# Three edits to a fused attention, soft-MoE and cosine-gated MLP kernel: the order of work where each of its stages opens or closes

## The chip, the cores and the metric

The kernel runs on one core of a Trainium2 chip. The metric is device time in microseconds (us) of one execution. A core has five engines that run their own instruction queues and wait for each other through semaphores: TensorE (PE; its weight loads are listed apart as PEld), VectorE (DVE), ScalarE (ACT), GpSimd (POOL) and SyncE (SP), which here only issues DMAs.

## The reference

```python
# q, k, v: (4, 12, 448, 64)
scores = np.where(causal_mask, -1e9, (q @ k.T) / 8)
attn = softmax(scores)                       # rows
x = (attn @ v)  -> (1792, 768)               # tokens x model
logits = x @ phi                             # 32 slots
slot_input = softmax(logits, axis=0).T @ x
for e in range(8):                           # 4 slots each
    slot_out[e] = relu(slot_input[e] @ w1[e]) @ w2[e]
x = softmax(logits, axis=1) @ slot_out
h = x @ w_in                                 # w_in, w_out: float64 on the host
out = (h * cos(h)) @ w_out                   # 768 -> 2048 -> 768
```

## The kernel before

**Three stages.** Attention works on 24 pairs of heads (`pair_step(t)`, L472, called for t = 0 to 26 in the loop at L595). The piece stage (L745 to L780) streams the expert weights w1 and w2 as 48 pieces of 1 MB. The last stage (L782 to L1004) computes h, h*cos(h) and the product with w_out. The instructions of one engine run in the order in which the code issues them (`tc.manual_schedule()`).

**Attention.** For a pair t the step issues the score products `qk_mm(t, c)` (L287), c = 0 to 2, two heads each, into banks 0 to 3 of PSUM. A fourth, small block of scores, c = 3, of both heads together, lies in the last 64 columns of bank 0 and is issued one step ahead, `qk_mm(t + 1, 3)` at L527. Dependencies are kept per bank, so the score products of a pair wait until DVE has read the c = 3 block out of bank 0. `score` (L298) is a DVE instruction that adds the mask (`cs`, a tile of constants: identity in columns 0 to 127, masks in 192 to 703, `rep` in 704 to 831) and takes the row maximum; it returns a function that issues the exponential on ACT (L308). Then come `recip` (L312), `norm` (L319, on DVE or POOL), and a step later the transposes (L328), their copies (L179, L181) and the product with v (L360 to L369). Before the first pair, L583 to L594 issue the loads of pair 0, of `cs`, of v of pair 0, of pair 1 and of phi on SP, five memsets on DVE, and the c = 3 block of pair 0 with its exponential.

**keep_warm(n)** (L457) issues n products of the identity with itself into bank 3. Nothing reads them. In float32 each product is two matmul records with two weight loads; every float32 product of this kernel shows so.

**The piece stage.** `next_piece` (L726) issues loads as slots come free. After the pieces come the loads of the raw weights of the last stage, `ld(j)` (L674): an item j is one 768 KB block of w_in (even j) or w_out (odd j), 128 of the 2048 hidden columns, in float64. There are four raw buffers, so ld(j) waits until item j - 4 has been decoded. `decode` (L697) turns float64 into float32 with one ACT instruction (L684) and three DVE ones, l (L687), h (L691) and s (L695). Item 0 is decoded inside the piece loop (L739). After the last piece the loop copies its sums (ACT L773), issues keep_warm(2), transposes (L778) and copies the result to `soT` (DVE L779).

**The last stage.** For a group q of hidden columns: `w_mm` (L790, product of soT and w_in, PE), `w_4` (L800, ACT), `w_rep` (L804, PE), `w_s` (L807, ACT), `w_d` (L811, DVE). Then for each of 64 steps s, a step being 128 hidden columns for a block of 512 (or 256) tokens: H (L827, PE), Y (L831, ACT), R (L834, DVE), S (L837, ACT), G (L840, DVE), K (L843, ACT: the high part of g), L (L846, POOL: the low part), and `back(s, m)` (L848): for each of six output blocks m three matmuls, high weight by high g (L853), low by high (L854) and high by low (L855). The high and low parts of w_out are made from item 2c + 1 by u (`up_part`, ACT L706) and v (`lo_part`, POOL or DVE L719). F copies or adds finished sums (L861 to L865). `SEQ` (L30) gives the order of blocks and columns: step 0 needs column block 0, step 1 block 1, step 4 block 2, step 8 block 3.

**The planner.** The order in which the last stage is issued comes from a list scheduler in the kernel's own Python (L871 to L983). Each task has the engines it may run on with a cost, its predecessors, and a key (its due time in steps); `free` holds when each engine is free, all 0.0. At a moment each free engine takes the ready task with the lowest key, unless a more urgent one becomes ready soon. Loads are tasks of 1.87 us, `("so",)` stands for soT, ready at 3.0. The plan decides order only; on the chip each engine waits where an input is late. After it, `warm` (L991) adds 6, 5 and 12 identity products behind the first w_mm, w_rep and H.

## Time and profile before

| | us |
|---|---|
| median of three runs (558.65 to 562.61) | 560.85 |
| the profiled execution | 561.64 |
| its span, first to last instruction | 559.9 |
| busy in the span: PE | 516.5 |
| DVE | 369.7 |
| ACT | 318.6 |
| POOL | 159.2 |

All times in the rows are microseconds from the start of the span; mean durations are ns. The profiled execution's own time is 1.74 us above its span. A matmul record starts when its data enters the array and ends with a modelled end, so records of one engine overlap, and the distance from one start to the next is what an instruction costs in a stream.

### The profile page before, as it was taken

To read this page: it belongs to the slowest core of one execution; us is meant where nothing else is said; L and a number is where in the kernel's file an instruction comes from. 1 tells how busy PE (TensorE), PEld (TensorE's weight loads), DVE (VectorE), ACT (ScalarE), POOL (GpSimd) and SP (SyncE) were. 2 spreads that over 40 slices of the span, in tenths; PEclk is the share of its full clock that TensorE was granted. 3 is DMA by queue.
4 is the path that set the end of the run, shared out by engine and by line. 5 is a ranking of instruction groups with operands and counts; after the bars stand their busy time and mean duration, and the time that the engine had idled before them with its cause. 6 is when DMAs were issued, how large, how long until landed. Compare 5 with 4: busy or idle time off the path is not lost.

```text
span 559.9 us, 10301 instructions
## 1 busy us (share of the span) xinstructions
PE 516.5 (92%) x3794; PEld 387.3 (69%) x3794; DVE 369.7 (66%) x918; ACT 318.6 (57%) x737; POOL 159.2 (28%) x195
## 2 busy tenths in 40 slices
PE   4999999989999998887779989999989999999997
PEld 2777767767767763422457768777867878888997
DVE  3777777778777745001488888788888987635532
ACT  4888858857886712001375866565647646543452
POOL 1233333323323300000053624342423422232231
PEclk9999999999999999998789999999999999999999
DMA  5477547475645689999844141424226101303301
GB/s 180 167 258 258 184 155 252 172 248 179 235 166 219 248 325 414 420 418 420 332 156 176 50 170 60 167 76 151 101 72 221 57 10 48 112 1 113 114 1 57
DMA packets 23954, 100.28 MB, mean 179 GB/s; under 512 B 2656, under 2 KB 6624, under 8 KB 17760
## 3 DMA queue, kind: packets, MB, share of 16 engines
q1 hardware_dynamic: 23904, 99.63, 47.8%
q8 instruction: 30, 0.49, 0.3%
q14 instruction: 20, 0.16, 0.1%
HBM read 94.11 MB, written 5.51 MB: 178 GB/s over the span
## 4 chain that ended last, share of the span: by engine, by line
PE 51%; DMA 19%; DVE 13%; ACT 12%; issue 3%; SPq 0%; ACTq 0%; DVEq 0%
DMA w<-in_w_dram 10%; PE bank L853 8%; PE bank L854 8%; PE bank L855 8%; PE bank L295 7%; PE bank L328 5%; ACT p L308 5%; DMA zraw<-in_w_in_dram 5%; DMA zraw<-in_w_out_dram 4%; ACT pts L179 3%; DVE zscr L840 2%; PE bank L827 2%; PE bank L363 1%; DVE zfa L695 1%; PE bank L390 1%
## 5 line engine op out<-in xcount | busy, mean ns | idle before, releaser
L853 PE MATMUL bank<-zg,zhl 128*128 128x512 f32 (+1 forms) x384 | 142.4, 371 | 0.0
L855 PE MATMUL bank<-zg,zhl 128*128 128x512 f32 (+1 forms) x384 | 140.2, 365 | 0.4 <-POOL zg L846 0.4
L854 PE MATMUL bank<-zg,zhl 128*128 128x512 f32 (+1 forms) x384 | 140.3, 365 | 0.0
L846 POOL TENSOR_TENSOR zg<-zscr,zg 128x512 fp32r<-128x512 f32 (+1 forms) x64 | 81.6, 1278 | 155.4 <-ACT zg L843 124.3
L308 ACT ACTIVATE p<-p,pst 128x320 f32<-128x320 f32 (+3 forms) x168 | 87.6, 526 | 32.5 <-DVE pst L306 30.6
L325 POOL TENSOR_SCALAR p<-p,pst 128x320 f32<-128x320 f32 (+3 forms) x120 | 62.6, 539 | 131.2 <-ACT p L308 116.4
L853 PEld LDWEIGHTS bank<-zg,zhl 128*128 128x128 f32 x384 | 73.0, 190 | 12.7 <-issue 1.4
L855 PEld LDWEIGHTS bank<-zg,zhl 128*128 128x128 f32 x384 | 72.9, 190 | 12.7 <-POOL zg L846 0.9
L854 PEld LDWEIGHTS bank<-zg,zhl 128*128 128x128 f32 x384 | 73.0, 190 | 11.4
L306 DVE CUSTOM_DVE_ANT_0 p<-bank,cs 128x320 f32<-128x320 f32 (+3 forms) x168 | 66.9, 448 | 16.4 <-PE bank L295 12.6
L328 PE MATMUL bank<-cs,p 128*128 128x128 f32 (+1 forms) x456 | 59.8, 277 | 3.1 <-ACT pts L179 2.9
L834 DVE SCALAR_TENSOR_TENSOR zscr<-zscr,bank 128x512 f32<-128x512 int32 (+1 forms) x64 | 39.4, 618 | 34.1 <-ACT zscr L831 33.7
L837 ACT ACTIVATE zscr<-zscr,b_h 128x512 f32<-128x512 f32 (+1 forms) x64 | 42.6, 669 | 27.7 <-DVE zscr L834 27.5
L328 PEld LDWEIGHTS bank<-cs,p 128*128 128x128 f32 (+1 forms) x456 | 49.6, 134 | 11.3 <-issue 9.5
L840 DVE TENSOR_TENSOR zscr<-bank,zscr 128x512 f32<-128x512 f32 (+1 forms) x64 | 39.6, 621 | 22.0 <-ACT zscr L837 21.8
L295 PE MATMUL bank<-qk 64*128 64x192 f32 (+2 forms) x288 | 48.3, 471 | 5.4 <-DVE pst L306 5.4
L843 ACT ACTIVATE zg<-zscr 128x512 fp32r<-128x512 f32 (+1 forms) x64 | 36.8, 576 | 28.6 <-DVE zscr L840 28.3
L831 ACT ACTIVATE zscr<-bank,b_q 128x512 int32<-128x512 f32 (+1 forms) x64 | 40.2, 630 | 22.1 <-PE bank L827 21.9
L295 PEld LDWEIGHTS bank<-qk 64*128 64x128 f32 x288 | 27.2, 196 | 26.3 <-issue 10.3
L179 ACT ACTIVATE pts<-bank 128x512 f32<-128x512 f32 x71 | 40.5, 591 | 3.8 <-PE bank L328 2.3
L684 ACT ACTIVATE zraw<-zraw 128x768 f32<-128x768 f32 x32 | 28.9, 910 | 23.4 <-DMA zraw<-in_w_in_dram 15.6
L719 POOL TENSOR_TENSOR zhl<-uacc,zhl 128x768 fp32r<-128x768 f32 x4 | 8.8, 2204 | 98.6 <-ACT zhl L706 98.6
(147 smaller groups left out, 692.6 us busy)
## 6 DMA issues: line engine op xcount, KB each, us to landing
w<-in_w_dram SPq DMA_DIRECT2D x48, 1024.0 KB, 6.9
zraw<-in_w_in_dram SPq DMA_DIRECT2D x16, 768.0 KB, 5.0
zraw<-in_w_out_dram SPq DMA_DIRECT2D x16, 768.0 KB, 4.4
qk<-in_qk_dram SPq DMA_DIRECT2D x24, 480.0 KB, 4.2
xk<-in_v_dram SPq DMA_DIRECT2D x12, 256.0 KB, 2.6
out_dram<-zps SPq DMA_DIRECT2D x8, 256.0 KB, 2.0
xts<-in_v_dram SPq DMA_DIRECT2D x12, 128.0 KB, 2.1
lt<-in_v_dram SPq DMA_DIRECT2D x12, 128.0 KB, 2.2
```

The source lines that it names most:

```text
L179: ACT.activation(o, i, AF.Copy)
L295: PE.matmul(sreg(j, c), lhsT=Q(p)[h, q0:q0 + 128], rhs=K(p)[h, 0:ln], start=True, stop=True)
L306: DVE.tensor_tensor_reduce(out=dst, in0=sb, in1=m, scale=-0.125, scalar=3.0e38, op0=ALU.add, op1=ALU.min, accum_out=st_[:, col:col + 1])
L308: return pr(f"exp{j}{c}")(lambda: ACT.activation(dst, dst, AF.Exp, bias=st_[:, col:col + 1], scale=-1.0, accum_out=st_[:, 8 + col:9 + col]))
L325: ENG[CFG["norm"][3 * j + c if c < 3 else 6]].tensor_scalar(dst, dst, st_[:, 24 + col:25 + col], 0.0, op0=ALU.mult, op1=ALU.add)
L328: PE.transpose(out, src, by)
L837: ACT.activation(y_(s), y_(s), AF.Sin, bias=b_h, scale=1.0)
L840: DVE.tensor_tensor(y_(s), hb[:, 0:n_(s)], y_(s), ALU.mult)
L846: eng.tensor_tensor(g_(s)[1], y_(s), g_(s)[0].bitcast(F32), ALU.subtract)
L853: PE.matmul(o, lhsT=wh, rhs=gh, start=first, stop=False)
L854: PE.matmul(o, lhsT=wl, rhs=gh, start=False, stop=False)
L855: PE.matmul(o, lhsT=wh, rhs=gl, start=False, stop=last)
```

## The change

Three edits. (1) In attention, the c = 3 block of pair 0 no longer comes first: the three main score products of pair 0 do, after eight identity products on a zeroed part of `uacc` into bank 7. Inside step 0, the c = 3 blocks of pairs 0 and 1 and the load of pair 2 are issued at new places, with 6 and 4 such products behind them. The load of `cs` becomes three, masks first. (2) In the piece loop, three identity products follow each of the pieces that are counted 42 to 47, and `decode(1)` is issued after the last piece, ahead of the copy that leads to soT. (3) The planner of the last stage starts from times at which the engines, soT and the first raw items are ready; loads cost 2.4 instead of 1.87; keys of w_in items are 0.7 step later; the twelve tasks from the first w_mm to the first output product (`CHN`) are a chain, and PE, ACT and DVE refuse any other task that would run past the moment at which the chain next needs that engine; identity products fill PE's gaps in the chain; and step 0's output products run as three passes over the six blocks (high by high; low by high; high by low), each pass with its own inputs.

```diff
-    def keep_warm(n):
+    def keep_warm(n, t=cs):
         for _ in range(n):
-            PE.matmul(bank[3][:, 0:128], lhsT=ident, rhs=ident, start=True, stop=True)
+            PE.matmul(bank[3 if t is cs else 7][:, 0:128], lhsT=t[:, 0:128], rhs=t[:, 0:128], start=True, stop=True)
...
-        if t + 2 < NPAIR:
+        if 0 < t < NPAIR - 2:
             load_raw(t + 2)
         sc(0, 0)
+        if t == 0:
+            qk_mm(0, 3)
+            keep_warm(6, uacc)
+            load_raw(2)
...
+        if t == 0:
+            e3 = score(0, 0, 3)
         sc(0, 1)
         sc(1, 1)
         e(1, 0)
+        if t == 0:
+            e3()
...
         sc(1, 2)
+        if t == 0:
+            qk_mm(1, 3)
+            keep_warm(4, uacc)
+            f3 = score(1, 0, 3)
...
-        if nxt:
+        if nxt and t:
             qk_mm(t + 1, 3)
...
-            e3 = score(t + 1, 0, 3)
+            e3 = score(t + 1, 0, 3) if t else f3
...
-        SP.dma_start(cs, cst)
+        SP.dma_start(cs[:, 192:704], cst[:, 192:704])
+        SP.dma_start(cs[:, 0:192], cst[:, 0:192])
+        SP.dma_start(cs[:, 704:832], cst[:, 704:832])
...
-        qk_mm(0, 3)
-        score(0, 0, 3)()
+        DVE.memset(uacc[:, 0:128], 0.0)
+        keep_warm(8, uacc)
...
+                    if 42 <= npc[0] < 48:
+                        keep_warm(3)
+                if npc[0] == 48:
+                    decode(1)
                 ACT.activation(so, sb[:, 0:256], AF.Copy)
                 tb = bank[6]
                 if npc[0] == 48:
-                    keep_warm(2)
+                    keep_warm(1)
...
+    def back0(s, m):
+
+        k_ = (0, 1, None, None, None, 2)[m]
+        gh, gl = g_(0)
+        for m in range(6):
+            fc = seq[0][1]
+            PE.matmul(bank[m][:, 0:n_(0)], lhsT=w_blk(fc, int(k_ == 1), m), rhs=gl if k_ == 2 else gh, start=k_ == 0,
+                      stop=k_ == 2 and seq[0][3])
...
-        key = need[GRP[qof[c]][0]] - 2.2 if k_ == "i" else need[c] - 0
-        if j >= 1:
+        key = need[GRP[qof[c]][0]] - 1.5 if k_ == "i" else need[c] - 0
+        if j == 1:
+            task(("s", 1), dict(DMA=5.05), [], -2)
+        if j >= 2:
             if j >= NRAW:
-                task(("ld", j), dict(DMA=1.87), [("s", j - NRAW) if j > NRAW else None], j)
+                task(("ld", j), dict(DMA=2.4), [("s", j - NRAW) if j > NRAW else None], j)
...
-    task(("so",), dict(DMA=3.0), [], -1)
+    task(("so",), dict(DMA=5.199999999999999), [], -1)
...
+        if s == 0:
+            task(("B", 0, 0), dict(T=1.4), [("K", 0), ("u", 0)], .0)
+            task(("B", 0, 1), dict(T=1.4), [("B", 0, 0), ("v", 0)], .1)
+            task(("B", 0, 5), dict(T=1.4), [("B", 0, 1), ("L", 0)], .2)
...
-    free = dict.fromkeys("TADP", 0.0)
+    free = dict(T=6.0, A=5.6, D=5.95, P=3.0)
+    TIMED = {("so",): 0, ("s", 1): 0, ("raw", 2): 0, ("raw", 3): 0}
+    for t, x in ((("raw", 2), 4.9), (("raw", 3), 6.8)):
+        T[t] = (dict(DMA=x - .9),) + T[t][1:]
+    CHN = [("wm", 0), ("w4", 0), ("wr", 0), ("ws", 0), ("wd", 0), ("H", 0), ("Y", 0), ("R", 0), ("S", 0), ("G", 0), ("K", 0), ("B", 0, 0)]
+    isch = set(CHN)
+
+    def chain_next(e, now):
+        # returns when the first unplanned task of CHN that runs on e is expected to be ready
...
+                if e in "TAD" and t not in isch and chain_next(e, now) < now + eng[e] - 0.05:
+                    continue
...
+                if e == "T" and ("wm", 0) in done and ("B", 0, 0) not in done and chain_next("T", now) > now + .3 and \
+                        not any(w_ < now + .3 and "T" in T[x][0] for w_, x in soon):
+                    plan.append((now, len(plan), ("kw",), e))
+                    free["T"] = now + .23
...
-    warm = {("wm", 0): 6, ("wr", 0): 5, ("H", 0): 12}
...
+            if t[0] == "kw":
+                keep_warm(1)
+                continue
```

(The comment line in `chain_next` stands for its body, which walks the chain with the planner's own costs.)

## Rows read from the trace of the kernel before

**Rows 1.** The chain that ended last, share of the span by line.
```profile
DMA w<-in_w_dram 10%; PE bank L853 8%; PE bank L854 8%; PE bank L855 8%; PE bank L295 7%; PE bank L328 5%; ACT p L308 5%; DMA zraw<-in_w_in_dram 5%; DMA zraw<-in_w_out_dram 4%; ACT pts L179 3%; DVE zscr L840 2%; PE bank L827 2%; PE bank L363 1%; DVE zfa L695 1%; PE bank L390 1%
```
**Rows 2.** Windows: length, busy PE, PEld, DVE, ACT, POOL (instructions), PE clock, DMA share, GB/s.
```profile
27.50:34.65 7.15, 6.82 (x57) 5.17 (x57) 5.61 (x23) 5.80 (x19) 2.59 (x6) 1.00 0.74 253
...
288.40:336.40 48.00, 44.71 (x223) 35.01 (x224) 41.75 (x54) 33.81 (x54) 21.18 (x14) 0.96 0.37 132
...
368.80:460.00 91.20, 86.72 (x450) 68.66 (x449) 78.89 (x108) 52.69 (x81) 30.45 (x21) 1.00 0.28 98
```
**Rows 3.** Timeline of the opening: start, duration, engine, line, instruction, idle before.
```profile
1.55 0.06 DVE L592 MEMSET b_h<- 128x1 f32 x1
...
3.99 0.69 PE L290 MATMUL bank<-qk 128*128 128x64 f32 x2 [3.99 <-DMA qk<-in_qk_dram]
...
5.68 3.50 PE L295 MATMUL bank<-qk 64*128 64x448 f32 x12 [1.00 <-DVE pst L306]
...
12.08 3.31 PE L295 MATMUL bank<-qk 64*128 64x448 f32 x12 [2.54 <-DVE pst L306]
...
20.57 1.89 PE L295 MATMUL bank<-qk 64*128 64x448 f32 x12 [0.18 <-DVE pst L306]
```
**Rows 4.** Windows with the granted clock, columns as in rows 2.
```profile
12.50:13.00 0.50, 0.50 (x4) 0.28 (x2) 0.33 (x2) 0.00 (x0) 0.50 (x2) 0.50 0.53 180
...
16.00:16.50 0.50, 0.50 (x7) 0.50 (x5) 0.50 (x3) 0.28 (x1) 0.00 (x0) 1.00 0.25 54
...
288.00:292.00 4.00, 3.75 (x10) 2.98 (x11) 3.38 (x6) 3.82 (x7) 3.01 (x3) 0.61 0.51 197
```
**Rows 5.** DMA issues from 2.0 to 2.5: the load of pair 1, us to landing.
```profile
qk<-in_qk_dram SPq DMA_DIRECT2D x1, 480.0 KB, 6.2
```
**Rows 6.** DMA issues from 253 to 254 (at 253.77): item 1, us to landing.
```profile
zraw<-in_w_out_dram SPq DMA_DIRECT2D x1, 768.0 KB, 19.2
```
**Rows 7.** Timeline from the last piece to the first output product.
```profile
271.26 1.89 PE L771 MATMUL bank<-w,dk 128*4 128x256 f32 x16 [0.71 <-DMA w<-in_w_dram]
...
273.08 0.93 PEld L459 LDWEIGHTS bank<-cs 128*128 128x128 f32 x4 [0.86 <-issue]
...
273.27 0.38 ACT L773 ACTIVATE cs<-bank 128x256 f32<-128x256 f32 x1 [9.19 <-PE bank L771]
273.56 0.89 ACT L684 ACTIVATE zraw<-zraw 128x768 f32<-128x768 f32 x1
...
274.76 0.19 DVE L779 COPY dT<-bank 128x32 f32<-128x32 f32 x1 [7.85 <-PE bank L778]
...
275.01 0.71 PE L794 MATMUL bank<-zfa,dT 128*32 128x128 f32 x12 [0.28 <-DVE dT L779]
275.53 0.96 DVE L691 SCALAR_TENSOR_TENSOR uacc<-zraw,uacc 128x768 int32<-128x768 int32 x1
...
275.77 0.28 ACT L802 ACTIVATE cs<-bank 128x128 f32<-128x128 f32 x1
...
278.78 2.60 POOL L719 TENSOR_TENSOR zhl<-uacc,zhl 128x768 fp32r<-128x768 f32 x1 [84.51 <-ACT zhl L706]
...
280.04 1.76 DVE L687 TENSOR_SCALAR lt<-zraw 128x768 int32<-128x768 int32 x1
...
284.04 0.29 DVE L813 TENSOR_TENSOR zWS<-bank,zWS 32x128 fp32r<-32x128 f32 x1 [1.52 <-ACT zWS L809]
...
284.38 0.49 PE L827 MATMUL bank<-CT,zWS 96*128 96x512 f32 x1 [0.69 <-DVE zWS L813]
...
285.29 0.68 ACT L831 ACTIVATE zscr<-bank,b_q 128x512 int32<-128x512 f32 x1
...
288.23 0.63 ACT L843 ACTIVATE zg<-zscr 128x512 fp32r<-128x512 f32 x1 [0.18 <-DVE zscr L840]
...
288.59 0.40 PE L853 MATMUL bank<-zg,zhl 128*128 128x512 f32 x1
```
**Rows 8.** The chain in order of time: start, length, one output product in a stream.
```profile
292.40 0.23 PE bank L853
```

More of the change, by code (lines that the diff above doesn't have):

```diff
@@ L895, in moe_stack_kernel @@
             task(("v", c), dict(P=1.9, D=.9), [("u", c)], key - .6, True)
-    task(("so",), dict(DMA=3.0), [], -1)
+    task(("so",), dict(DMA=5.199999999999999), [], -1)
     for q, grp in enumerate(GRP):
-        key = need[grp[0]] - 2.2
+        key = need[grp[0]] - 1.5
         n = len(grp)
@@ L914, in moe_stack_kernel @@
         task(("L", s), dict(P=.07 + 1.2 * w, D=.07 + .55 * w) if LD else dict(P=.07 + 1.2 * w), [("K", s)], s - 1.5, True)
+        if s == 0:
+            task(("B", 0, 0), dict(T=1.4), [("K", 0), ("u", 0)], .0)
+            task(("B", 0, 1), dict(T=1.4), [("B", 0, 0), ("v", 0)], .1)
+            task(("B", 0, 5), dict(T=1.4), [("B", 0, 1), ("L", 0)], .2)
         for m in range(6):
+            if s == 0:
+                if last:
+                    task(("F", s, m), dict(D=.61) if m % 2 == 0 else dict(A=.5), [("B", 0, 5)], s + .2 + m / 10)
+                    pb[m] = ("F", s, m)
+                continue
             pv_ = ("B", s, m - 1) if m else (("B", s - 1, 5) if s else None)
@@ L927, in moe_stack_kernel @@
             succ.setdefault(x, []).append(t)
-    free = dict.fromkeys("TADP", 0.0)
+    free = dict(T=6.0, A=5.6, D=5.95, P=3.0)
[5 more added lines that the diff above has]
+    def chain_next(e, now):
+        w = None
+        for x in CHN:
+            if x in done:
+                continue
+            d = [y for y in T[x][1] if y not in done]
+            if not d:
+                r = tr_[x]
+            else:
+                r = max([tr_[x]] + [est_.get(y, now) for y in d])
+            (xe, dur), = [(k_, v_) for k_, v_ in T[x][0].items()][:1]
+            if xe == e:
+                return r
+            est_[x] = max(now, r, free[xe]) + dur + LAT[xe]
+        return 1e9
+    done, est_ = set(), {}
     free["DMA"] = 0.0
@@ L932, in moe_stack_kernel @@
     pool, plan, hbf, hbo, now = [], [], [0.0, 0.0], {}, 0.0
-    while len(plan) < len(T):
+    while len(done) < len(T):
         pool += [t for w_, t in soon if w_ <= now + 1e-9]
@@ L948, in moe_stack_kernel @@
                     continue
+                if e in "TAD" and t not in isch and chain_next(e, now) < now + eng[e] - 0.05:
+                    continue
                 if e in "TAD" and any(w_ < now + LA * eng[e] and T[x][2] < key - KD and e in T[x][0] for w_, x in soon):
@@ L954, in moe_stack_kernel @@
             if best is None:
+                if e == "T" and ("wm", 0) in done and ("B", 0, 0) not in done and chain_next("T", now) > now + .3 and \
+                        not any(w_ < now + .3 and "T" in T[x][0] for w_, x in soon):
+                    plan.append((now, len(plan), ("kw",), e))
+                    free["T"] = now + .23
+                    moved = True
                 continue
@@ L958, in moe_stack_kernel @@
             st_ = max(now, port["P" if e == "D" else "D"]) if pt and e in port else now
-            if t[0] == "so":
+            if t in TIMED:
                 fin = eng[e]
@@ L973, in moe_stack_kernel @@
             pool.remove(t)
+            done.add(t)
             plan.append((now if e != "DMA" else now, len(plan), t, e))
@@ L985, in moe_stack_kernel @@
     bk = lambda t: bank[6 + hbo[t]]
-    run = dict(ld=ld, a=dec_a, l=dec_l, h=dec_h, s=dec_s, u=up_part, S=t_s, K=t_k, B=back)
+    run = dict(ld=ld, a=dec_a, l=dec_l, h=dec_h, s=dec_s, u=up_part, S=t_s, K=t_k, B=lambda s, m: (back if s else back0)(s, m))
     run.update(H=lambda s: t_h(s, bk(("H", s))), Y=lambda s: t_y(s, bk(("H", s))), R=lambda s: t_r(s, bk(("H", s))),
@@ L990, in moe_stack_kernel @@
         run[nm] = lambda q, fn=fn: fn(q, bk(("wm", q)))
-    warm = {("wm", 0): 6, ("wr", 0): 5, ("H", 0): 12}
     with tc.manual_schedule():
         for _, _, t, e in plan:
-            if t[0] in ("so", "raw"):
+            if t in TIMED:
+                continue
+            if t[0] == "kw":
+                keep_warm(1)
                 continue
@@ L1003, in moe_stack_kernel @@
                 run[t[0]](*t[1:])
-            keep_warm(warm.get(t, 0))
 def _layout(inputs):
```

## The prediction, made before the changed kernel was run

> **What bounds the kernel now.** The reading goes from the chain that ended last, to the windows of each stage, to the timelines of the three places that the change touches. The chain [rows 1] shows the stages: score products (L295) and transposes (L328) with the exponentials for attention, 10% of waiting for expert pieces, and three lines of output products with 8% each, beside 9% of waits for raw weights. The windows [rows 2] give the bound of each. A step of attention (27.50 to 34.65) has PE busy for 6.82 of 7.15 us, so what its start wins is carried to its end. In the piece stage the PE waits for the transfer even of the last piece (0.71 idle before 271.26, [rows 7]), so pieces arrive a fixed time after attention frees their slots, and a win in attention passes through it unchanged. In the last stage PE is the bound, with gaps: 3.29 us idle in 288.4 to 336.4 and 4.48 in 368.8 to 460, 7.8 together; DVE is idle there for 6.25 and 12.31, 18.6 together. So PE comes first, DVE close behind it.
>
> The openings are where PE stands or runs slowly. In attention the twelve records of a pair's main scores take 3.50 and 3.31 us for pairs 0 and 1, and 1.89 for pair 2 [rows 3]; the granted clock of the second stretch is 0.50, 1.2 GHz, and 1.00 by 16.0, 3.9 us after the PE began to work at 12.08 [rows 4]. (The record gives 1.00 for the first stretch, but the durations are those of 0.50.) Between the end of soT (274.76 + 0.19 = 274.95) and the first output product (288.59) lie 13.64 us [rows 7].
>
> **Edit 1, attention.** Removed: the c = 3 block of pair 0 ahead of all, which waited for `cs` and held bank 0 until 5.68. Added ahead of pair 0: one small memset and 16 records of identity products. They start behind the memsets, about 1.65 [rows 3]. An identity record at the low clock costs 0.93 / 4 = 0.233 (weight loads at 273.08, [rows 7], where PE had not yet recovered), half of it, 0.117, at 2.4 GHz. So 16 end at 1.65 + 3.73 = 5.4. Scores could start at 3.99 (pair 0 has landed [rows 3]); they start at 5.5, hardly before 5.68. The masks are the second transfer as before and smaller, so I cost their arrival at nothing.
>
> What is won is the clock: by rows 4 it rises up to 3.9 us after work begins, here 5.5. Then scores of pair 0 run 5.5 to 7.4; the c = 3 block to 7.7; six products (12 x 0.117 = 1.4) to 9.1. Pair 1 landed at 2.1 + 6.2 = 8.3 [rows 5]; two more issues on SP ahead of it make it later by what no row gives, and 0.8 of room is there up to 9.1. Its c = 3 block ends at 9.5, four products (0.94) at 10.45, and the scores of pair 1 run 10.45 to 12.35, against 12.08 + 3.31 = 15.39: **3.0 us won**. DVE's read of pair 1's c = 3 block now stands before the normalisation in its queue: a late pair 1 would hold `recip` and `norm` behind it, but by 9.8 it is done, and exponentials end only then. The load of pair 2 waits for the c = 3 product, ends its wait near 7.7 and is wanted a step later; the loads of v and phi move back by the same two issues and are wanted steps later. From both sides: if the clock stays low throughout, 5.4 + 3.5 + 0.45 + 12 x 0.233 + 0.45 + 8 x 0.233 = 14.5, scores end at 17.8, 2.4 lost; if the scores began at 3.99 and all else followed, 4.5 won. I take 3.0, since the second work stretch of rows 4 is the nearest.
>
> **Edit 2, the end of the pieces.** Three products are 6 records: 1.40 at the low clock, 0.70 at the high. A piece comes each 1.89 + 0.71 = 2.60 and costs 1.89 low, about 0.95 high. High, 1.65 fits into 2.60; low, 3.29 doesn't, and PE would fall back 0.69 a piece, 4.1 over six. But a PE that never idles rose to 1.00 in rows 4, so I take 0, and keep 0 to 4.1. `decode(1)` lies on the path: item 1 lands at 253.77 + 19.2 = 272.97 [rows 6]. ACT's decode (0.89) now stands ahead of the copy that before began at 273.27; DVE's l, h and s stand ahead of soT. h starts at 273.9, s follows, 2 x 0.96 [rows 7] with 0.1 between: 275.9, soT at 276.1. That is **1.15 later** than 274.95, and no PE speed helps. In return item 1 is decoded, and its raw buffer free, 1.6 us earlier (h began at 275.53 before).
>
> **Edit 3, the chain of the last stage.** From soT on, by rows 7: w_mm 0.71, w_4 0.28, w_rep (a 128-column product; H's 0.49 as ceiling), w_s 0.28, w_d 0.29, H 0.49, each with 0.05 of handing over (275.72 to 275.77); then Y to K without other work between, 285.29 to 288.23 + 0.63, 3.57 for five. Sum 0.71 + 0.28 + 0.49 + 0.28 + 0.29 + 0.49 + 3.57 + 8 x 0.05 = 6.5. The rest of the 13.64 is queueing behind decoding, which the chain now refuses. The first output product comes at 276.1 + 6.5 = 282.6 instead of 288.59: **6.0 won** with edit 2's delay inside.
>
> The clock: 288 to 292 was granted 0.61 [rows 4], after PE had idled before 288.59. (1 - 0.61) / 0.5 x 4.0 = 3.1 us at 1.2 GHz cost 3.1 / 2 = **1.6**. The fillers keep PE at work in the chain, so I count it won (bounds 0 and 1.6).
>
> Given back: step 0's three passes last 18 x 0.23 = 4.1 [rows 8], to 286.7. Step 1 wants item 3's high and low parts and its own L. After G of step 0 (281.7) DVE still has w_d, h and s to do (0.29 + 2 x 0.96, to 284.0), ACT the high part (about 0.89), POOL the low (2.60, [rows 7]): 287.5, or near 286 if DVE takes it; then L on POOL. I charge **1.5** (0 to 2.7). Behind that DVE is later against PE than before: when step 1 began, it had before also two instructions each of items 4 and 6 and R and G of step 2, at most 4 x 0.96 + 2 x 0.71 = 5.3. Its 18.6 us of idle time hide this; without that cover it costs the 5.3. I charge **0.6**, near the lower end, for one late group.
>
> A rule bears on the gaps. The DVE shift at 280.04 lasted 1.76, though h on the same tile size takes 0.96, and ended 0.42 after the POOL instruction that ran from 278.78 for 2.60 [rows 7]. The Trainium skill, SBUF — State Buffer, section "Who interferes with whom", says that such a DVE instruction and a POOL one want a shared pair of ports, and that the second to come waits fully. By that rule a decoding step put into a gap beside POOL's low part holds the chain's next DVE instruction; by the row that is 1.76 - 0.96 = 0.8, and the sum would be 7.7. The planner's port check keeps most of it out, so the sum goes without.
>
> **Sum.** 3.0 + 6.0 + 1.6 - 1.5 - 0.6 = 8.5 off the profiled execution's 561.64: 553.1. That execution lies 0.8 above the median of 560.85, so the forecast is 552.3.
>
> **Rivals.** (a) DVE takes over as the bound: all 5.3 come back, the last stage keeps 0.8 + attention's 3.0 = 3.8, 557.0. For it: DVE is busy 87% in both windows of rows 2. Against: it still had 18.6 us of idle time. (b) The clock doesn't rise in the opening, so edit 1 doesn't do what it says: -2.4 instead of 3.0, 557.7. For it: the first twelve records stayed low for all their 3.5 us; against: rows 4. (c) Slower: w_in items come too late. Their keys move by 0.7 step, 0.7 x 4.1 = 2.9 us, and each of the seven later groups must pass w_mm to K, about 6.5, before its first output product. If PE waits 2.9 at each group, 20.3 - 8.5 = 11.8 are lost: 572.6; slower than before from 1.2 a group on. For it: PE already has 7.8 us of gaps, so the lead is small at places. Against: the higher load price (2.4) makes the plan put fewer instructions in front of data that hasn't landed, and keys matter only where DVE has a choice. (d) Better: the new plan also removes half of the 7.8: 548.4.
>
> **How the numbers follow.** Forecast 0.55, (a) 0.20, (b) 0.10, (c) 0.06, (d) 0.09. The forecast's own range, from the bounds on step 1 and the clock, is 549.5 to 555. The range for 8 in 10 takes in (a), (b) and (d): 546 to 559. About 1%, 5.6 us, is what a measurement of this kernel tells from no change; that is 555.2. Faster by more: nine tenths of the forecast, all of (d), a third of (a), a quarter of (b): 0.68. Slower by more: most of (c), 0.05. Within: 0.27.
>
> **What would show it.** Edit 1: the scores of pair 1 end near 12.4, the twelve records of pair 0 take about 1.9, and everything up to the last piece is 3 us earlier. Edit 2: granted clock 1.00 up to the last piece; soT 3.1 us after item 1 lands, against 2.0 before. Edit 3: soT to first output product 6.5, not 13.6, and no stretch at 0.50 in step 0. It is wrong if the time from the first output product to the end of the span grows by more than 3 us: then the plan, or DVE, gave the opening back; or if the last piece doesn't move.

## The result, and the profile of the changed kernel

The changed kernel takes 552.32 us (median of four runs, 551.28 to 552.65) against 561.16 in the same job: a ratio of 0.9851, 95% interval 0.9825 to 0.9876. The forecast of 552.3 was right. Its profiled execution took 552.22, with a span of 550.4.

The chain that ended last, share of the span by line (L871 to L873 are the output products, L845 is H, L459 the identity products):

```profile
PE bank L871 11%; PE bank L873 11%; PE bank L872 11%; DMA w<-in_w_dram 6%; PE bank L295 6%; ACT p L308 6%; PE bank L328 5%; DMA zraw<-in_w_out_dram 4%; ACT pts L179 3%; PE bank L845 2%; PE bank L459 2%; PE bank L770 1%; PE bank L363 1%; PE bank L390 1%; DVE p L306 1%
```

Against [rows 1] the three lines of output products grew from 8% to 11%: PE itself is the chain for longer. The waits for w_in, 5% before, are no longer on the list. The windows that answer to [rows 2], the same stretches after pair 0 and after the first output product:

```profile
24.70:31.85 7.15, 6.78 (x60) 5.44 (x59) 5.84 (x25) 6.00 (x20) 2.82 (x6) 1.00 0.76 257
282.00:330.00 48.00, 45.22 (x228) 34.40 (x227) 41.91 (x58) 36.75 (x58) 19.37 (x13) 1.00 0.36 132
362.30:453.50 91.20, 90.62 (x470) 72.38 (x469) 78.76 (x105) 53.34 (x84) 37.86 (x25) 1.00 0.29 101
```

Attention's step is unchanged. PE's idle time in the 48 us behind the first output fell from 3.29 to 2.78, and in the long window from 4.48 to 0.58. The forecast counted no win in these gaps; only its rival (d) did.

PE's timeline of the opening, answering to [rows 3]: start, duration, engine, line, instruction.

```profile
1.81 3.78 PE L459 MATMUL bank<-uacc 128*128 128x128 f32 x16 [1.81 <-DVE uacc L607]
5.52 2.48 PE L295 MATMUL bank<-qk 64*128 64x448 f32 x12
7.93 0.43 PE L290 MATMUL bank<-qk 128*128 128x64 f32 x2
8.20 1.56 PE L459 MATMUL bank<-uacc 128*128 128x128 f32 x12
...
9.76 1.11 PE L459 MATMUL bank<-uacc 128*128 128x128 f32 x8
10.80 1.89 PE L295 MATMUL bank<-qk 64*128 64x448 f32 x12
```

Pair 1's scores end at 12.69 (predicted 12.35, before 15.39), at 1.89 for twelve records; those of pair 0 took 2.48, between that and the 3.50 of [rows 3], so the clock rose within them (the prediction had them at about 1.9). The timeline from the last piece to the first output product, answering to [rows 7]:

```profile
268.87 1.05 PE L785 MATMUL bank<-w,dk 128*4 128x256 f32 x16 [0.57 <-DMA w<-in_w_dram]
...
270.72 0.90 ACT L698 ACTIVATE zraw<-zraw 128x768 f32<-128x768 f32 x1 [9.46 <-DMA zraw<-in_w_out_dram]
...
272.64 0.96 DVE L709 SCALAR_TENSOR_TENSOR uacc<-zraw,uacc 128x768 int32<-128x768 int32 x1
273.52 0.18 DVE L797 COPY dT<-bank 128x32 f32<-128x32 f32 x1
...
273.76 1.07 PE L812 MATMUL bank<-zfa,dT 128*32 128x128 f32 x12 [1.38 <-DVE dT L797]
...
274.76 1.22 PE L459 MATMUL bank<-cs 128*128 128x128 f32 x4
274.87 0.28 ACT L820 ACTIVATE cs<-bank 128x128 f32<-128x128 f32 x1 [1.35 <-PE bank L812]
...
275.77 0.63 PE L823 MATMUL bank<-cs 128*96 128x128 f32 x2
...
276.20 1.49 PE L459 MATMUL bank<-cs 128*128 128x128 f32 x6
...
276.75 0.29 DVE L831 TENSOR_TENSOR zWS<-bank,zWS 32x128 fp32r<-32x128 f32 x1 [0.53 <-ACT zWS L827]
277.07 0.56 DVE L701 TENSOR_SCALAR lt<-zraw 128x768 int32<-128x768 int32 x1
...
277.34 0.77 PE L845 MATMUL bank<-CT,zWS 96*128 96x512 f32 x1
277.53 1.81 POOL L733 TENSOR_TENSOR zhl<-uacc,zhl 128x768 fp32r<-128x768 f32 x1 [86.08 <-ACT zhl L720]
...
278.15 0.69 ACT L849 ACTIVATE zscr<-bank,b_q 128x512 int32<-128x512 f32 x1 [0.70 <-PE bank L845]
...
281.07 0.63 ACT L861 ACTIVATE zg<-zscr 128x512 fp32r<-128x512 f32 x1 [0.43 <-DVE zscr L858]
...
281.43 0.71 PE L845 MATMUL bank<-CT,zWS 96*128 96x512 f32 x2
...
281.98 4.27 PE L881 MATMUL bank<-zg,zhl 128*128 128x512 f32 x18
```

soT (L797) now ends 4.83 us after the last piece landed, and the first output product (L881) comes 8.28 after soT, not the predicted 6.5. Windows of the same stretch; the third number from the end is the granted clock, as in [rows 4]:

```profile
273.70:275.00 1.30, 1.24 (x13) 0.81 (x14) 1.20 (x3) 0.13 (x1) 0.00 (x0) 0.50 0.84 241
...
277.00:278.00 1.00, 1.00 (x5) 0.60 (x3) 0.60 (x2) 0.45 (x1) 0.47 (x1) 0.50 0.85 289
...
279.00:280.00 1.00, 1.00 (x7) 0.96 (x6) 1.00 (x2) 0.68 (x2) 0.34 (x1) 0.59 0.45 184
280.00:281.00 1.00, 1.00 (x12) 1.00 (x11) 0.68 (x2) 0.59 (x2) 0.00 (x0) 1.00 0.03 12
```

A granted clock of 0.50 is 1.2 GHz, so w_mm, w_rep and H ran at the lower level. Before that PE had stood 1.60 us and 1.38 us around the last transposes, while DVE decoded item 1; e4 below tests whether this standing is the reason.

The span by stages, in us; each mark is the start of a row like those above:

| | before | after | won | predicted |
|---|---|---|---|---|
| start to first piece product | 208.32 | 205.48 | 2.84 | 3.0 |
| first to last piece product | 62.94 | 63.39 | -0.45 | 0 |
| last piece product to soT | 3.69 | 4.83 | -1.14 | -1.15 |
| soT to first output product | 13.64 | 8.28 | 5.36 | 7.1 |
| first output product to the end | 271.31 | 268.42 | 2.89 | -0.5 |

The second line is the piece transfer and differs from one execution to the next (62.0 to 63.9 in the profiles of this study), so stages are compared below from the last piece to the end: 288.64 before, 281.53 after, 7.1 won. The third line differs too where nothing in it was changed: it is 3.69 here, but 2.83 and 2.92 in the profiles of e1 and e10, which have the old code there.

### The profile page after: what moved, and what is told of

Read it like the earlier page. It is cut to its first block, busy times and chain, and to the rows that moved or that the text cites. A ratio compares the mean times of both kernels' runs of the same rounds, so it can differ in the third digit from the quotient of the medians.

```text
span 550.4 us, 10404 instructions
## 1 busy us (share of the span) xinstructions
PE 519.9 (94%) x3844; PEld 392.8 (71%) x3844; DVE 366.2 (67%) x911; ACT 317.7 (58%) x737; POOL 165.3 (30%) x203
## 4 chain that ended last, share of the span: by engine, by line
PE 60%; ACT 13%; DVE 12%; DMA 11%; issue 3%; POOL 0%; ACTq 0%; SPq 0%
PE bank L871 11%; PE bank L873 11%; PE bank L872 11%; DMA w<-in_w_dram 6%; PE bank L295 6%; ACT p L308 6%; PE bank L328 5%; DMA zraw<-in_w_out_dram 4%; ACT pts L179 3%; PE bank L845 2%; PE bank L459 2%; PE bank L770 1%; PE bank L363 1%; PE bank L390 1%; DVE p L306 1%
## 5 line engine op out<-in xcount | busy, mean ns | idle before, releaser
L871 PE MATMUL bank<-zg,zhl 128*128 128x512 f32 (+1 forms) x378 | 139.7, 370 | 0.4 <-ACT zhl L720 0.4
L872 PE MATMUL bank<-zg,zhl 128*128 128x512 f32 (+1 forms) x378 | 137.5, 364 | 0.9 <-DVE zhl L733 0.9
L873 PE MATMUL bank<-zg,zhl 128*128 128x512 f32 (+1 forms) x378 | 137.2, 363 | 0.8 <-POOL zg L864 0.8
L864 POOL TENSOR_TENSOR zg<-zscr,zg 128x512 fp32r<-128x512 f32 (+1 forms) x64 | 82.8, 1298 | 138.7 <-ACT zg L861 122.8
L308 ACT ACTIVATE p<-p,pst 128x448 f32<-128x448 f32 (+3 forms) x168 | 87.6, 526 | 31.6 <-DVE pst L306 29.8
L871 PEld LDWEIGHTS bank<-zg,zhl 128*128 128x128 f32 x378 | 71.5, 189 | 13.7 <-ACT zhl L720 1.0
L872 PEld LDWEIGHTS bank<-zg,zhl 128*128 128x128 f32 x378 | 71.5, 189 | 12.4 <-DVE zhl L733 1.4
L873 PEld LDWEIGHTS bank<-zg,zhl 128*128 128x128 f32 x378 | 71.4, 189 | 12.5 <-POOL zg L864 1.3
L306 DVE CUSTOM_DVE_ANT_0 p<-bank,cs 128x448 f32<-128x448 f32 (+3 forms) x168 | 66.7, 448 | 14.3 <-PE bank L295 14.3
L295 PE MATMUL bank<-qk 64*128 64x192 f32 (+2 forms) x288 | 45.9, 451 | 1.8 <-DVE pst L306 1.8
L733 POOL TENSOR_TENSOR zhl<-uacc,zhl 128x768 fp32r<-128x768 f32 (+1 forms) x7 | 10.6, 1529 | 101.4 <-ACT zhl L720 101.4
```

Source lines behind the costliest of these rows:

```text
L295: PE.matmul(sreg(j, c), lhsT=Q(p)[h, q0:q0 + 128], rhs=K(p)[h, 0:ln], start=True, stop=True)
L306: DVE.tensor_tensor_reduce(out=dst, in0=sb, in1=m, scale=-0.125, scalar=3.0e38, op0=ALU.add, op1=ALU.min, accum_out=st_[:, col:col + 1])
L308: return pr(f"exp{j}{c}")(lambda: ACT.activation(dst, dst, AF.Exp, bias=st_[:, col:col + 1], scale=-1.0, accum_out=st_[:, 8 + col:9 + col]))
L864: eng.tensor_tensor(g_(s)[1], y_(s), g_(s)[0].bitcast(F32), ALU.subtract)
L871: PE.matmul(o, lhsT=wh, rhs=gh, start=first, stop=False)
L872: PE.matmul(o, lhsT=wl, rhs=gh, start=False, stop=False)
```

## The experiments

"Opening" is soT to the first output product, "tail" the last piece product to the end, both of one profiled execution. A median is that of 4 to 12 executions, beside the kernel before in the same job. The intervals reach about 0.25% to either side, 1.4 us, and two rows of the table come from different jobs in most cases, so medians less than some 2 us apart are not told apart by them alone.

| run | median (before) | ratio, 95% | opening | tail |
|---|---|---|---|---|
| changed kernel | 552.32 (561.16) | 0.9851, 0.9825 to 0.9876 | 8.28 | 281.53 |
| e1 attention alone | 557.49 (560.98) | 0.9925, 0.9898 to 0.9953 | 13.89 | 288.87 |
| e2 no products behind pieces | 551.80 (560.98) | 0.9821, 0.9792 to 0.9851 | 7.84 | 280.84 |
| e3 chain ahead of item 1 | 561.74 (560.98) | 1.0007, 0.9987 to 1.0028 | 14.59 | 291.64 |
| e4 PE kept at work | 551.41 (560.98) | 0.9821, 0.9791 to 0.9851 | 8.21 | 281.68 |
| e3b as e3, item 4 priced | 553.92 (560.87) | 0.9873, 0.9849 to 0.9896 | 6.54 | 282.71 |
| e5 no products in attention | 553.40 (560.87) | 0.9865, 0.9833 to 0.9896 | 7.56 | 282.30 |
| e6 old price and keys | 554.19 (560.87) | 0.9894, 0.9867 to 0.9922 | 7.79 | 285.53 |
| e7 no refusal | 552.42 (560.87) | 0.9850, 0.9824 to 0.9876 | 8.91 | 282.81 |
| e8 new price, old keys | 558.68 (560.92) | 0.9958, 0.9937 to 0.9979 | 8.35 | 292.79 |
| e9 load priced 3.7 | 546.25 (560.92) | 0.9747, 0.9721 to 0.9773 | 7.77 | 276.21 |
| e10 price and keys on the kernel before | 557.75 (560.92) | 0.9938, 0.9920 to 0.9956 | 13.89 | 284.19 |
| e11 as e3b, load priced 3.7 | 549.52 (561.01) | 0.9793, 0.9776 to 0.9810 | 6.55 | 278.27 |

### Attention (e1, e5)

e1 is the kernel before with all of edit 1 and nothing else; its core:

```diff
-        qk_mm(0, 3)
-        score(0, 0, 3)()
+        DVE.memset(uacc[:, 0:128], 0.0)
+        keep_warm(8, uacc)
```

> The kernel before with edit 1 alone. If the edits add up (theory), the scores of pair 1 end near 12.7 as in the changed kernel, the first piece's products start 2.8 us earlier than before (205.5 instead of 208.3), the last piece lands 2.4 to 2.8 earlier, the last stage runs as before, and the total is 558.5 to 558.8 beside 561.2. Rival: the last stage, held by decoding, takes it back, and the total stays within 0.5 of 561.2.

The theory held: 3.5 us by the median, and the first piece product at 205.02, 3.3 earlier than before; the tail of 288.87 is that of the kernel before (288.64). Edit 1 is worth what was forecast and is carried through the piece stage. e5 is the changed kernel without the identity products of attention, with the new order kept:

```diff
-            keep_warm(6, uacc)
...
-            keep_warm(4, uacc)
...
-        keep_warm(8, uacc)
```

> The changed kernel without the identity products in attention (8, 6 and 4); order and loads as changed. Theory (they win the clock): pair 0's scores run at the low clock from 4.0 to 7.5, pair 1's also, 9.8 to 13.1 instead of 10.8 to 12.7, and the total is 0.4 above the changed kernel's. Rival (the order alone wins, and the scores bring the clock up by themselves): pair 1's scores run 9.8 to 11.7, and the total is about 1.0 below the changed kernel's.

PE's timeline of its opening:

```profile
4.03 3.57 PE L295 MATMUL bank<-qk 64*128 64x448 f32 x12 [4.03 <-DMA qk<-in_qk_dram]
...
10.06 3.57 PE L295 MATMUL bank<-qk 64*128 64x448 f32 x12 [0.83 <-DVE pst L306]
...
19.58 1.89 PE L295 MATMUL bank<-qk 64*128 64x448 f32 x12 [0.18 <-DVE pst L306]
```

The same place of the changed kernel, pair 2:

```profile
17.97 1.89 PE L295 MATMUL bank<-qk 64*128 64x448 f32 x12 [0.18 <-DVE pst L306]
```

The scores of pairs 0 and 1 run at the low clock, though those of pair 0 begin 1.5 us sooner than in the changed kernel. The scores of pair 2 begin at 20.57 before [rows 3], at 19.58 here and at 17.97 in the changed kernel: the order alone wins 1.0 there, and the products, by the clock, another 1.6. The first piece product comes at 207.08, again 1.6 later than with the products, which leaves 1.2 of the 2.84 for the order. (That mark lies anywhere from 204.43 to 205.78 in the profiles that have all of edit 1.) The medians are 1.1 apart, where 0.4 was expected, and don't settle it by themselves.

### The end of the pieces (e2)

```diff
-                    if 42 <= npc[0] < 48:
-                        keep_warm(3)
```

> The changed kernel without the eighteen identity products behind pieces 42 to 47. Theory: soT hangs on the landing of item 1 and its decoding, so soT still ends 3.0 us after that landing although the last pieces' products run at the low clock, and the total is within 0.7 of 552.3. Rival: the products are what makes edit 2 pay; the last piece's products take 1.9 instead of 1.05, soT is 0.8 later, the chain is slower at the low clock, and the total is 553.1 or more.

The theory held. soT comes 4.86 after the last piece, as with the products, and the median is not above that of the changed kernel. Without the products the last three pieces take 1.89, 1.57 and 1.05 us on PE instead of 1.05 each, so they keep the clock up, but soT waits for the decoding of item 1 and not for PE, and nothing is bought with them.

### Is the late opening the clock, and does an early one pay? (e4, e3, e3b)

e4 adds identity products around the last transposes, so that PE doesn't stand there:

```diff
                 if npc[0] == 48:
-                    keep_warm(1)
+                    keep_warm(7)
...
+                if npc[0] == 48:
+                    keep_warm(5)
```

> The changed kernel with seven instead of one identity products ahead of the last transposes and five behind them. Theory (the chain took 8.3 us instead of 6.5 because PE, idle from 270.3 on, was at 0.50 up to 279.6): the granted clock stays at 1.00 from the last piece through the chain, soT ends at the same time, the first output product follows 6.5 to 7 us after it, 1.3 to 1.8 earlier. With PE as the bound behind it the total is 550.7 to 551.2; rival, with step 1 held by item 3's parts, the total stays within 0.5 of 552.3.

The granted clock was 1.00 from the last piece through the whole opening, so PE's standing was the reason for its fall. w_mm took 0.63 instead of 1.07, yet the opening is 8.21 against 8.28, not the 6.5 to 7 expected. The tail is the same too (281.68), and the median, 0.9 lower, decides between neither of the two totals. The timeline shows what took the clock's place:

```profile
274.95 1.82 POOL L733 TENSOR_TENSOR zhl<-uacc,zhl 128x768 fp32r<-128x768 f32 x1 [83.94 <-ACT zhl L720]
275.01 2.18 DVE L701 TENSOR_SCALAR lt<-zraw 128x768 int32<-128x768 int32 x1
...
275.56 0.69 ACT L851 ACTIVATE zscr<-bank,b_q 128x512 int32<-128x512 f32 x1 [0.70 <-PE bank L847]
...
277.22 0.69 DVE L854 SCALAR_TENSOR_TENSOR zscr<-zscr,bank 128x512 f32<-128x512 int32 x1
```

With the chain earlier, item 3's shift (L701) falls behind the start of POOL's low part instead of ahead of it. It takes 2.18 instead of 0.56, and R (L854), next on DVE, starts at 277.22 though Y ended at 276.25: 0.97 lost. Another 0.5 goes to s of item 2, which stands ahead of w_d on DVE. In the changed kernel the shift at 277.07 began 0.46 before POOL and took 0.56. The Trainium skill, SBUF — State Buffer, section "Who interferes with whom", says that of a DVE instruction that uses the ports shared with POOL and a POOL one, whichever is issued first holds them for all of its time and the other blocks fully. The trace agrees at both places: in e4 the shift ended 0.42 after POOL (277.19 against 276.77), in the changed kernel, issued first, it took no longer than alone.

e3 issues the chain ahead of item 1: `decode(1)` goes back into the plan, and the plan's starts become those of the earlier soT.

```diff
-                if npc[0] == 48:
-                    decode(1)
...
-    task(("so",), dict(DMA=5.199999999999999), [], -1)
+    task(("so",), dict(DMA=2.4), [], -1)
...
-    free = dict(T=6.0, A=5.6, D=5.95, P=3.0)
+    free = dict(T=3.1, A=2.7, D=3.3, P=3.0)
...
```

> The changed kernel with decode(1) out of the piece loop: soT comes first, item 1 is decoded by the plan in the gaps of the chain, and the plan's start times are set to that. Theory (soT was held 2.7 us by item 1, and PE's idling there made the chain slow): soT ends about 2.1 us after the last piece lands instead of 4.8, the granted clock stays at 1.00, the first output product follows 6.5 to 7 us later, some 4 us earlier than in the changed kernel, and PE, as the bound behind it, carries most of that to the end: 548.5 to 550. Rival (the decoding on DVE binds what follows): step 1 waits for item 3's parts until the time at which it starts now, and the total stays within 0.7 of 552.3.

soT came 2.5 earlier, as expected, but the opening took 14.59. One row of DVE says why:

```profile
275.41 0.56 DVE L701 TENSOR_SCALAR zfb<-zraw 128x768 int32<-128x768 int32 x1 [4.90 <-DMA zraw<-in_w_in_dram]
```

The plan had put l of item 4 ahead of w_d, taking that load to be there at 3.3. It wasn't; DVE stood 4.90 us with the chain queued behind. The experiment had failed for a reason of its own, so e3b prices this one load by what it takes while the pieces still fill the queue:

```diff
-                task(("ld", j), dict(DMA=2.4), [("s", j - NRAW) if j > NRAW else None], j)
+                task(("ld", j), dict(DMA=2.4 if j > NRAW else 7.8), [("s", j - NRAW) if j > NRAW else None], j)
```

> As e3, with one number mended: the plan believed that item 4 lands 3.3 into its time, while it landed 5.3 us later, so DVE stood 4.9 us at its shift ahead of w_d. Item 4 is now planned for the time at which it landed. Theory (soT was held by item 1, and PE is the bound behind the chain): soT ends 2.1 us after the last piece lands (4.8 in the changed kernel), the first output product comes 9 to 9.5 after that landing instead of 13.1, and the time from landing to the end of the span is 277.5 to 279.5 instead of 281.5. Rival (decoding on DVE and item 3's landing set step 1, whatever the chain does): the first product is earlier but landing to end stays at 281 to 282.

The opening is 6.54: the chain as the prediction added it up, 6.5, without a stall. The first output product comes 8.82 after the last piece instead of 13.11, 4.3 earlier. The end doesn't follow: the tail is 282.71 against 281.53, where 277.5 to 279.5 was expected, and the median lies 1.6 above the changed kernel's. DVE and PE of this run:

```profile
276.78 2.22 DVE L701 TENSOR_SCALAR lt<-zraw 128x768 int32<-128x768 int32 x1
279.03 1.94 DVE L705 SCALAR_TENSOR_TENSOR lt<-zraw,lt 128x768 int32<-128x768 int32 x1
```

```profile
280.49 1.64 PE L879 MATMUL bank<-zg,zhl 128*128 128x512 f32 x6
283.04 0.73 PE L843 MATMUL bank<-CT,zWS 96*128 96x512 f32 x2 [0.90 <-DVE zWS L829]
286.88 0.79 PE L843 MATMUL bank<-CT,zWS 96*128 96x512 f32 x1 [3.12 <-DVE zscr L856]
287.83 0.79 PE L869 MATMUL bank<-zg,zhl 128*128 128x512 f32 x1 [0.16 <-ACT zg L859]
```

Step 0's passes end at 282.1, and the next output product comes at 287.83. Item 3 still has to be decoded at the first output, and two of DVE's three instructions for it, the rows above, are held beside POOL, which makes item 1's low part (276.09 for 2.48) and then step 0's low part of g (278.54 for 1.62). PE's clock falls in the wait, to 0.57 on average from 285 to 288. What sets the rate here is the supply of step 1, and a chain that runs earlier only moves the standing from ahead of the first output to behind it; e11 below repeats this with another price.

### What is won behind the first output? (e7, e6, e8, e10, e9, e11)

e7 takes the chain's refusal out of the planner:

```diff
-                if e in "TAD" and t not in isch and chain_next(e, now) < now + eng[e] - 0.05:
-                    continue
```

> The changed kernel without the rule that refuses tasks which would run into the chain; start times, prices and the three passes stay. Theory (the chain was long before because decoding stood ahead of it): the time from soT to the first output product goes from 8.3 back to 11 to 13.6, and the total rises by 2 to 4. Rival (the start times alone give the order): soT to first output product stays near 8.3 and the total within 0.7.

The same time (552.42), an opening 0.6 longer: with the start times in place, the plan keeps nearly the same order without the rule (from the last piece on POOL's is the same, DVE's differs at 23 of 294 places). The theory that the refusal carries edit 3 fell. e6 and e10 test two numbers of the plan; e6 sets them back in the changed kernel, e10 puts them alone into the kernel before.

```diff
-        key = need[GRP[qof[c]][0]] - 1.5 if k_ == "i" else need[c] - 0
+        key = need[GRP[qof[c]][0]] - 2.2 if k_ == "i" else need[c] - 0
...
-                task(("ld", j), dict(DMA=2.4), [("s", j - NRAW) if j > NRAW else None], j)
+                task(("ld", j), dict(DMA=1.87), [("s", j - NRAW) if j > NRAW else None], j)
...
```

(The key of the groups, further down, goes from 1.5 to 2.2 in the same way.)

> The changed kernel with the load price of 1.87 and the keys of w_in items and groups at 2.2 as before; the chain and the start times stay. Theory (PE's waits behind the first output product fell from 7.7 to 5.2 because loads are priced nearer to their landing): the waits return to 7 or more, the time from the first output product to the end of the span is 1.5 to 2.6 longer than 268.4, and the total is 1.5 to 2.6 above the changed kernel's. Rival (the lead of the chain does it): total and waits within 0.7 of the changed kernel's.

> The kernel before with the two numbers of the plan alone, load price 2.4 and keys 1.5; no start times, no chain, no edit to attention or pieces. Theory (price and keys are a gain of their own, 4 of the 7.1 that edits 2 and 3 win from landing to end): landing to end falls from 288.6 to 284.5 to 286, total 557 to 559. Rival (they pay only behind an early first product): total within 0.9 of 561.

Set back, they cost 1.9 by the median (no execution of e6 was as fast as any of the changed kernel) and 4.0 in the tail. Alone on the kernel before they win 3.2 by the median and 4.4 in the tail, with its opening of 13.89 untouched. Both theories held, with a little more in the tail than expected. So of what edits 2 and 3 win, 5.2 by the medians (557.49 to 552.32) and 7.1 in the tail, between a third and six tenths comes from two numbers that have nothing to do with the opening.

The two numbers change more than the places of loads. The low parts of w_out are made by whichever of POOL and DVE the plan chooses, and of the 24 instructions for them DVE has 17 in the kernel before and in e6, but 9 in the changed kernel and 8 in e10. How much of the gain is DVE's relief and how much the loads was not separated.

e8 has the new price with the old keys (the first of e6's two lines, and its twin further down):

> The changed kernel with the keys of w_in items and groups back at 2.2 and the load price kept at 2.4; e6 had both back and was 1.9 slower, with 4.0 more from the landing of the last piece to the end of the span (285.5 against 281.5). Theory (the price does it, since loads land 4.3 to 5.2 us after their issue and the plan lets ACT and DVE run into them): the total is within 0.7 of the changed kernel's 552.3 and landing to end 281 to 282.5. Rival (the keys do it, since they let DVE make w_out parts first): landing to end 284 to 286 and a total near 554.2.

6.4 worse than the changed kernel: the price without the keys is worse than neither (e6) by 4.5. Both theory and rival missed. In the tail its PE waited 11.5 us behind the first output, against 5.2 in the changed kernel and 7.1 in e6. ACT's waits for loads don't explain this: they are 17.5 here and 19.4 in e6, which is faster.

```profile
ACT zraw L698 <- DMA zraw<-in_w_in_dram: 11.1, 8, 2.4
ACT zraw L698 <- DMA zraw<-in_w_out_dram: 6.4, 6, 2.1
```

Why price and keys need each other was not taken apart; DVE again has 18 of the 24 low parts here. The landing times, which the price stands for, are in the trace: DMA issues from 300 to 440 of the changed kernel, median us to landing.

```profile
zraw<-in_w_out_dram SPq DMA_DIRECT2D x10, 768.0 KB, 4.3
zraw<-in_w_in_dram SPq DMA_DIRECT2D x10, 768.0 KB, 4.3
```

The plan takes a load to be there 0.9 after its price: 3.3 in the changed kernel, 2.8 before. The price is also the shortest distance between two loads in the plan, so a new price changes two things at once. e9 makes the landing 4.6, a little more than those 4.3:

```diff
-                task(("ld", j), dict(DMA=2.4), [("s", j - NRAW) if j > NRAW else None], j)
+                task(("ld", j), dict(DMA=3.7), [("s", j - NRAW) if j > NRAW else None], j)
```

> The changed kernel with the load price at 3.7, which with the plan's 0.9 of handing over is the 4.6 that loads took from issue to landing. Theory (each plan order that counts on a load too early makes an engine stand in its queue): ACT's waits for loads fall below the 13.9 of the changed kernel, PE's waits behind the first output product below 5.2, landing to end 279 to 281, total 550 to 551.8. Rival (what is left is latency of the steps themselves): the total stays within 0.7 of 552.3.

546.25, the best of all: another 6.1 off by one number, where 0.5 to 2.3 was expected. The waits on ACT (line, what for: us in total, times, longest), of the kernel before, the changed kernel and e9 in turn, each from the first output on:

```profile
ACT zraw L684 <- DMA zraw<-in_w_in_dram: 15.1, 10, 2.8
...
ACT zraw L684 <- DMA zraw<-in_w_out_dram: 7.8, 6, 2.1
```

```profile
ACT zraw L698 <- DMA zraw<-in_w_in_dram: 12.3, 9, 3.3
...
ACT zraw L698 <- DMA zraw<-in_w_out_dram: 1.6, 3, 0.7
```

```profile
ACT zraw L698 <- DMA zraw<-in_w_in_dram: 4.5, 3, 3.1
...
ACT zraw L698 <- DMA zraw<-in_w_out_dram: 0.5, 2, 0.3
```

22.9, 13.9 and 5.0 us: ACT stood at a load that the plan had put too early in its queue, with K, Y and S of the next steps behind it. PE's waits behind the first output fall with them, 9.2, 5.2 and 2.6. That is 2.6 of the 4.8 us by which this stretch is shorter in e9 (263.6 against 268.4). What was predicted of the waits came true, but that they are the cause is not shown: e8 and e6 don't follow them, any new price shuffles the order of the whole stage, and no other price near 3.7 was run. Windows of e9:

```profile
330.10:440.00 109.90, 109.75 (x556) 88.51 (x555) 100.27 (x134) 70.06 (x108) 47.17 (x28) 1.00 0.33 114
440.00:530.00 90.00, 90.00 (x513) 78.14 (x512) 49.21 (x86) 45.94 (x86) 28.62 (x29) 1.00 0.17 62
```

From 330 on PE idles for 0.15 us in 200. What is left to win in the last stage lies in front of that. e11 asks whether e3b's early chain pays once the loads are priced right; it is e3b with 3.7 in place of 2.4:

> The run that put the chain ahead of item 1 had its first output product 4.3 us earlier than the changed kernel and ended its last stage 1.2 later; the run that priced a load at 3.7 ended it 5.3 earlier. Both edits together. If what follows the first output is bounded by the supply of step 1 whatever the loads are priced at, the last landing to the end takes about 276.2 + 1.2 = 277.4 us, a time near 547.5. If only the wrong price of the loads wasted the early first output, its 3.8 us (12.6 to 8.8) are carried to the end: 272.4 us, near 542.5. In both cases soT to first output is near 6.5.

278.27 and 549.52: the first theory's side (277.4 and 547.5), even a little worse, and 2.1 more in the tail than e9. Against e3b the price of 3.7 wins 4.4 by the medians, the second case in which it pays with the new keys. The opening was 6.55, and between the last pass of step 0 and the first product of step 1 PE again stood 3.05 us for DVE, where the same two instructions were held beside POOL (2.21 and 1.93 for 0.55 and 0.96, 2.6 too long). The early opening doesn't pay in either plan. Even with those 2.6 given back, which was not tried, the tail would be 275.7, only 0.5 below e9's for a first output product 3.8 us nearer to the last piece.

## Why the prediction was right, and which of its steps were not

**Edit 1: right in size, its reason in part.** 2.84 of 3.0. "What is won is the clock" holds for 1.6 of it (e5); the other 1.2 comes from the new order, also at the low clock, a term that the sum doesn't have. Pair 0's records took 2.48 and not about 1.9.

**Edit 2: right.** soT came 1.14 later against 1.15, and 2.98 after ACT could begin on item 1, against 3.1. The close match is partly luck: against the old code in e1 and e10 (2.83 and 2.92 for 3.69) the same 4.83 is 1.9 to 2.0 later. The products behind the pieces cost nothing, as taken, and by e2 bring nothing.

**Chain, 6.5: mis-sized by 1.8.** The sum of the twelve instructions is right, as e3b shows (6.54). In the changed kernel w_mm took 1.07 for 0.71 and H 0.77 for 0.49 at the low clock, the identity products delayed w_rep by 0.6 and H by 0.3 (each lasts twice as long there), w_rep took 0.63, and two other H stood ahead of the first output. The step that failed is "The fillers keep PE at work in the chain": PE had lost its clock before the chain began, behind `decode(1)`, a cost that edit 2 was not charged with. The clock did come back by 281, so the 1.6 for step 0 was won. Where it is held (e4), a wait beside POOL (0.97) and an instruction ahead of w_d (0.5) take its place. The prediction priced such a wait at 0.8 and left it out of the sum; the price itself is too low, since it takes 0.96 as the shift's own time, which is 0.55, so that its row says 1.2. That "the chain now refuses" the decoding is not what made the opening short: without the refusal (e7) it is only 0.6 longer.

**Step 1, -1.5: right.** PE stood 0.36 and 0.94 for its high and low parts, 1.3 together.

**"Behind that DVE is later against PE than before", -0.6: the step that failed.** The stage behind the first output won 2.89. With 1.6 for the clock and -1.3 for step 1 that leaves +2.6 in place of the -0.6. The argument carried the old plan forward with a later DVE, but the new price and keys change the order of the whole stage, and they alone win 4.4 in the tail of the kernel before (e10). By what they win it is not settled. ACT's standing at loads fell from 22.9 to 13.9, a number that the prediction didn't read, and DVE, which it took to be later, lost 8 of its 17 low parts to POOL. It named the first, "fewer instructions in front of data that hasn't landed", only as an argument against rival (c). Rival (d), which got 0.09, came true in this term: of the 7.8 of gaps in the two windows 4.4 went. Rival (c) had the sign of the keys wrong: at the new price the changed kernel loses 6.4 without their 0.7 step (e8). Rivals (a) and (b) did not occur.

**"6.0 won" at the first output product, carried to the end: not borne out.** 4.2 of the 6.0 came, 5.36 less 1.14 in the table above. e3b and e11 bring the first output 4.3 and 3.8 us nearer and end no earlier than the kernels they are compared with. How much of the 7.1 in the tail is due to the opening stays open: e10 accounts for 4.4, and the other 2.7 (2.0 by the medians) is split between the start times, the three passes and item 1's early decoding, which were not tried one by one.

So the total was right partly by luck, as two errors of opposite sign nearly cancel. Edit 1 won 0.2 less than forecast, the pieces took 0.45 more, the chain won 1.8 less and what follows it 3.4 more. Together the span won 9.5 instead of 8.5, and the profiled execution before happened to lie above its median while the one after doesn't, so 8.8 is left between the medians.

## What to carry to other kernels

Where a static order is planned from prices, compare each price with the trace early: a load that the plan takes to be there too soon puts a waiting instruction at the head of an in-order queue, and here a load price of 3.7 instead of 2.4 was worth 6.1 us, more than the 5.4 of the opening. Then measure, since a single price is no rule: from 1.87 to 2.4, also nearer to the landing, but with the old keys, it cost 4.5. Before a stall is shortened, ask what supplies the work behind it; if that is late too, the stall only moves. When one cause of a delay is removed and the time stays, look for the next one at the same place, as the wait beside POOL behind the low clock here. And compare a win with how much the same stretch differs between executions of unchanged code, as the way to soT did (2.83 to 3.69).

## What the runs showed of the hardware

DVE's shift (L701 now, L687 before) on a 128x768 tile takes 0.55 alone. Issued behind the start of a POOL tensor_tensor and held by it, it ended 0.41 to 0.43 after POOL's end: 281.80 against 281.38 in [rows 7], 277.19 against 276.77 in e4, 279.00 against 278.57 in e3b, 279.63 against 279.22 in e11. All 66 shifts of the fourteen profiles that overlap such an instruction begun earlier and take 0.6 or more end so, and all 43 that began first took 0.54 to 0.57, so which of the two starts first decides, by as little as 0.06 us (e4). The scalar_tensor_tensor behind it (0.96 alone) took 1.94 in e3b beside POOL's next instruction. The other way round, POOL's low part, 1.81 in the changed kernel, took 2.60 [rows 7] and 2.48 (e3b) where such a DVE instruction had begun just before it. A 768 KB load in the last stage landed after 4.3 us, though item 1, issued behind the pieces, needed 19.2 [rows 6].
